# Split weights kept in DRAM and loaded again for every later use of their unit

## The chip, the cores and the metric

The kernel runs on one core of one Trainium2 chip. The metric is the device time of one execution in microseconds, lower is better. The core has TensorE (PE in the profile, with its weight loads as PEld), VectorE (DVE), ScalarE (ACT), GpSimd (POOL) and SyncE (SP); in this kernel SP issues every DMA, in the order of the program. A difference under 0.2% (2.6 us) is about what a measurement of this kernel cannot tell from none.

## The reference, cut to what matters

```
x  = linear_attention(q, k, v)                      # 4 batches, 8 heads, 576 tokens, 64 per head
p  = domain_probs / (sum(domain_probs) + 1e-9)      # [2304, 4]
y  = sum over e of p[:, e] * (relu(x @ w1[e]) @ w2[e])   # w1[e] [512, 1024], w2[e] [1024, 512], float32
h  = y @ w_in                                       # w_in [512, 2048], float64
out = (h * sigmoid(1.702 * h)) @ w_out              # w_out [2048, 512], float64; out [2304, 512]
```

x is attention's result as 2304 tokens of 512 features. The two layers after it, a mixture of four experts and a gated feed-forward layer, are nearly all of the products. The weights of the second layer arrive as float64 and are turned into float32 on the chip.

## The kernel before, in words

**Products.** A float32 operand is split into two float32r parts, `hi` (a rounded copy, made by ACT) and `lo` (operand minus `hi`, made by POOL or DVE); a product is hi*hi + hi*lo + lo*hi, three matmuls. The first product of a layer runs on 2 x 2 blocks with seven block products (Strassen's scheme in Winograd's form), so a unit of weights needs seven pieces: `a11`, `a12`, `a22`, taken from the loaded block, and `s1` to `s4`, sums and differences that POOL makes first (`sum_w`, line 481). `hi_w1` and `lo_w1` (lines 486, 490) split them; `hi_w2` and `lo_w2` (lines 494, 498) split the two halves of the second product's weights.

**Units, passes, steps.** Weights come in units of 256 hidden columns: 16 units for the experts, 8 for the feed-forward layer. Only half of the tokens (two batches, a pass) fits at once, so each layer goes over all of its units twice. A pass has two pairs of token blocks (2 x 256 and 2 x 320 tokens), and a step is one unit on one pair: the seven block products, the activation, and between them the second product of the step before. The first three units run on the first pair alone before the second pair is there, and are prepared again for the second pair. So there are 51 preparations (`insts`; 3 + 32 + 16) for 24 different units: 24 first ones and 27 repeats. Every preparation loads 1 MiB (`load_w`: `ra` and `rc`, 512 KiB each), makes four sums, seven splits and two splits, all anew.

**Order.** The opening (`START`) is a hand-written list of pieces in the order of issue. Then `step` runs five stages per step: pieces of the first product, a tile of the second product of the step before, the preparation of the next unit's weights (`prepare`, with the plan `TWO`), the second product's own weights (`hi_w2`, `lo_w2` in stages 1 and 3 of a unit's first step), and one turn of background work (`pump`). Background work is attention for the second pass's tokens during the experts' first pass, and `decode_all` during their second pass: 32 pieces of float64 weights, each loaded by SP (`w64`), turned into float32 by seven DVE operations and one POOL operation (lines 511 to 531) over four turns, and stored by SP to DRAM (line 532). The next piece's load is issued in the first of a piece's four turns, the store at the end of the last. The program's order is kept up to the second unit of the feed-forward layer (`AUTO`); after that Tile, the layer under the kernel, orders the instructions.

**Buffers.** Split pieces of the first product have 20 half-piece buffers (`w1p`), those of the second 8 (`w2p`); loaded blocks have 3 (`rawp`).

Of the kernel before, what the change touches and what calls it, by code (L numbers as in the profile page):

```python
# [8 lines left out]
F32 = mybir.dt.float32  # L9
BF16 = mybir.dt.bfloat16  # L10
F32R = mybir.dt.float32r
# [11 lines left out]
def tile_linear_attention_moe_gelu(  # L23
# [11 lines left out]
):  # L35
    """Linear attention, a mixture of experts and a gated feed-forward layer.

    A float32 operand of a product is the exact sum of two float32r parts of 12 bits, hi and lo;
    a product is hi*hi + hi*lo + lo*hi, three passes. The first product of each layer runs
    on 2 x 2 blocks with seven block products (Winograd's form of Strassen's scheme).  # L40

    Tokens of a batch are taken in the order c * 96 + p for token p * 6 + c. A pass covers two
    batches; weights come in units of 256 columns of the hidden layer.
    """
    nc = tc.nc
# [3 lines left out]
    NT, DM = out.shape  # L49
# [19 lines left out]
    accp = ctx.enter_context(tc.tile_pool(name="accp", bufs=TT))  # L69
    w1p = ctx.enter_context(tc.tile_pool(name="w1p", bufs=20))  # L70
    w2p = ctx.enter_context(tc.tile_pool(name="w2p", bufs=8))
    rawp = ctx.enter_context(tc.tile_pool(name="rawp", bufs=3))
# [38 lines left out]
    def probs_ops():  # L111
        """The normalized probabilities, each on its token's partition, as pieces by name.

        They come as [p, b, c, e]; a product with a shifted identity puts the token c * 96 + p
        into its tile of 128.
        """
        y = {}

        def pr_(_):
            n = evp.tile([SP, B, NCH, E], F32, tag="ev", name="prn")  # L120
            sh = evp.tile([SP, 3 * SP], F32, tag="ev", name="shift")
            sm = evp.tile([SP, B * NCH], F32, tag="ev", name="prs")
            y.update(sh=sh, sm=sm, f=n.rearrange("p b c e -> p (b c) e"))
            S_.dma_start(
                out=n.rearrange("p b c e -> p b (c e)"),
                in_=probs.rearrange("(b p c) e -> p b (c e)", b=B, c=NCH),
            )
            G.memset(sh, 0.0)
            G.tensor_copy(sh[:, SP : 2 * SP], ident[:SP, :SP])

        def pn(_):
            sm, f = y["sm"], y["f"]
            V.tensor_reduce(out=sm, in_=f, op=ALU.add, axis=AX.X)
            V.tensor_scalar_add(sm, sm, EPS)
            V.reciprocal(sm, sm)
            V.tensor_tensor(
                out=f, in0=f, in1=sm.unsqueeze(2).to_broadcast([SP, B * NCH, E]), op=ALU.mult
            )

        def pp(_):  # L140
            f, sh = y["f"], y["sh"]
            ps = y["ps"] = pso.tile([P, NT // P, E], F32, tag="o", name="pr_ps")
            by_tile = ps.rearrange("p (x t) e -> p x t e", t=3)
            by_group = f.rearrange("p (x g) e -> p x g e", g=4)
            for t in range(3):
                first = [(0, *divmod(t * P, SP))]
                first += [((g * SP) - t * P, g, 0) for g in range(4) if t * P < g * SP < (t + 1) * P]
                for x, (o, g, p0) in enumerate(first):
                    T.matmul(
                        by_tile[:, :, t, :], sh[:, SP + p0 - o : SP + p0 - o + P], by_group[:, :, g, :],  # L150
                        start=(x == 0), stop=(x == len(first) - 1), skip_group_check=True,
                    )

        def pc(_):
            V.tensor_copy(pr, y["ps"])

        return {"pr": pr_, "pn": pn, "pp": pp, "pc": pc}

# [1 line left out]

    KT_PATH = (0,)  # batches whose k takes its maximum on its transpose
    AHEAD = 3  # units that run on the first pair of tokens before the second is there
    LEAD = 5
# [28 lines left out]
    def attend(b, j, pool, bufs, x, small_bufs):  # L192
        """Softmax of a pair of heads and its product, x transposed into xf: its pieces by name.

        The maximum and the exponential of k are taken on k (k..) or on its transpose (K..).
        x has the tiles of k, q and v.
        """
        nm = f"{b}_{j}"
# [166 lines left out]
    def attention(todo, pool, skew):  # L365
        """Every turn a piece of each pair of heads begun; a new one every skew turns."""
        load = lambda b, j: (b, j, {x: load_attn(x, b, j, pool, 5, 2) for x in "kqv"})
# [14 lines left out]

# [1 line left out]

    X = {}

    def blocks(i, nm):
        """The seven blocks of xf[i] the products take, as pieces by name; the sums are made in place."""
        n = PAIRS[i][1]
# [31 lines left out]
    def blocks_x(g, i):  # L421
        """The blocks of the next pass, some in every stage of the steps in between."""
        ops = blocks(i, f"g{g}")
        for x in BLOCK_STAGES:
            run(ops, x)
            yield

    def to_x2(g, ti):
        """One tile of tokens of the layer's result, transposed into xf."""
        src = acc[ti]  # L430
# [10 lines left out]

# [1 line left out]

# [9 lines left out]
    insts = [*range(AHEAD), *range(NG)]  # L453
    raw, W1, W2 = {}, {}, {}

    def load_w(m, part):
        kind, e, f, *_ = units[insts[m]]
        cols = slice(f * FU, (f + 1) * FU)
# [18 lines left out]

    def sum_w(m, x):
        l, r, op = MADE[x]
        o = sump.tile([P, 2, P], F32, tag="s", name=f"{x}_{m}")  # L480
        G.tensor_tensor(out=o, in0=block_w(m, l), in1=block_w(m, r), op=op)  # L481
        sums[m, x] = o

    def hi_w1(m, x):
        W1[m, x] = tuple(w1p.tile([P, 2, P], F32R, tag="w1", name=f"{x}{r}{m}") for r in "hl")
        A.copy(W1[m, x][0], block_w(m, x))  # L486

    def lo_w1(m, x, eng):
        hi, lo = W1[m, x]
        eng.tensor_tensor(out=lo, in0=block_w(m, x), in1=hi.bitcast(F32), op=ALU.subtract)  # L490

    def hi_w2(m, c):
        W2[m, c] = tuple(w2p.tile([P, DM], F32R, tag="w2", name=f"w2{r}{m}_{c}") for r in "hl")
        A.copy(W2[m, c][0], raw[m, 1][:, c, :])  # L494

    def lo_w2(m, c, eng):
        hi, lo = W2[m, c]
        eng.tensor_tensor(out=lo, in0=raw[m, 1][:, c, :], in1=hi.bitcast(F32), op=ALU.subtract)  # L498

    def decode(src, dst, pool, nm):  # L500
        """float64 bits to the nearest float32, beyond its range clamped by the exponent."""
        n = src.shape[1]
# [28 lines left out]
        G.tensor_tensor(out=o, in0=o, in1=t.bitcast(F32), op=ALU.add)  # L531
        S_.dma_start(out=dst, in_=o)
        yield

# [1 line left out]

# [13 lines left out]
    def mm1(g, i, m, ho):  # L550
        """The first product of a layer on one block of tokens and its activation, as pieces by name."""
        n = PAIRS[i][1]
# [63 lines left out]

    # the pieces of mm1 in five stages; the last two entries run in the next step's first stage
    STAGES = {
# [5 lines left out]
    def mm2(g, ti, m, ho):  # L624
        """One tile of tokens of the second product, and its sum: as two pieces."""
        kind, e, f, pas, first, last = units[g]
# [41 lines left out]

    # what becomes of the next weights during the stages of a step, over two steps or over one
    TWO = (  # L670
# [13 lines left out]

    # the program's order is kept up to the feed-forward layer; there Tile orders it
    AUTO = 2 * NPASS * len(moe) + 2
# [18 lines left out]
    def decode_all(dec):  # L705
# [10 lines left out]
        for n, x in enumerate(todo):  # L716
            if n + 1 < len(todo):
                next(todo[n + 1])
            yield from x

    def step(k_, tiles, tail):
        """mm1 of one unit on one pair, between it the tiles of mm2 of the step before."""
        g, i, m = steps[k_]
# [34 lines left out]

    # The beginning up to the second step of the second pair, in the order of issue: piece:whose@engine;
    # _b_j is a pair of heads, a number alone a unit's weights, b a pair's blocks, s a step.  # L760
    # A bare number is so many products that keep TensorE's clock up.
    START = """
# [53 lines left out]
    def keep_warm(n):  # L816
        """TensorE's clock drops when it idles; it is kept up through the waits of the beginning."""
        for _ in range(n):
            T.matmul(hot, warm, warm, start=True, stop=True)
# [96 lines left out]
```

## Time and profile before

| | |
|---|---|
| three timed runs | 1308.29, 1309.29, 1311.00 us; median 1309.29 |
| profiled execution, first to last instruction (its own time) | 1308.0 us |
| busy: PE, PEld | 1243.1 us (95%), 1097.3 us (84%) |
| busy: DVE, ACT, POOL | 1018.5 us (78%), 585.6 us (45%), 715.4 us (55%) |
| chain of work that ended last | PE 62%, DVE 31%, issue 3%, POOL 2%, ACT 1% |
| moved by DMA | 98.85 MB, mean 76 GB/s |

Busy times of the engines overlap. The span falls into an opening (up to about 140 us), the experts' first pass (to 477), their second (to 898), and the feed-forward layer's two passes (to 1104, and to the end); where one pass gives over to the next, new blocks of the moving operand are made. A row of the view by windows gives, for one stretch, the busy time of each engine with the count of its instructions, the granted TensorE clock as a share of full speed, the mean busy share of the DMA engines, and what they moved. Matmuls are pipelined and their ends are modelled, so PE busy all the time can still be PE below its best rate.

### The profile page before, as it was taken

The page shows a single profiled execution, that of the slowest core. Times are in us where ns is not written, and L with a number is a line of the kernel's source. Part 1 is how long each engine was busy: PE and PEld are TensorE (multiplying, and loading weights), DVE is VectorE, ACT ScalarE, POOL GpSimd, SP SyncE. Part 2 cuts the span into 40 slices and gives each one's busy share as a digit, 9 for nine tenths or more (in the row PEclk, how much of TensorE's full clock was granted, in tenths as well). Part 3 has the DMA queues.
Part 4 walks back from the last instruction along what each step waited for, and adds up shares of the span by engine and source line. Part 5 has one row for each costly group of instructions (what it writes and reads, how often), then busy time and mean ns, then how long its engine had stood idle before and what let it go on. Part 6 is the DMA issues. An engine that isn't in the chain of part 4 may idle for free.

```text
span 1308.0 us, 20206 instructions
## 1 busy us (share of the span) xinstructions
PE 1243.1 (95%) x7313; PEld 1097.3 (84%) x7313; DVE 1018.5 (78%) x1721; ACT 585.6 (45%) x1468; POOL 715.4 (55%) x755
## 2 busy tenths in 40 slices
PE   8788999999999998999999999999999998999998
PEld 7677888889888987888878787898799996899997
DVE  7997776666676587999999999758666669566765
ACT  4564344344433455433333333335754555654542
POOL 5686545444454475756665566547653558354430
PEclk9899999999999998999999999999999999999999
DMA  9324222222210112334433333111120112220102
GB/s 196 104 65 125 59 76 60 60 76 77 60 49 33 49 65 81 105 121 118 125 113 115 111 121 105 65 49 33 49 65 33 50 49 65 73 65 33 40 10 73
DMA packets 82899, 98.85 MB, mean 76 GB/s; under 512 B 27760, under 2 KB 59248, under 8 KB 82800
## 3 DMA queue, kind: packets, MB, share of 16 engines
q1 hardware_dynamic: 82800, 97.57, 25.8%
q8 instruction: 57, 0.93, 0.3%
q14 instruction: 42, 0.34, 0.1%
HBM read 84.45 MB, written 13.11 MB: 75 GB/s over the span
## 4 chain that ended last, share of the span: by engine, by line
PE 62%; DVE 31%; issue 3%; POOL 2%; ACT 1%; SPq 1%; DMA 0%; POOLq 0%; DVEq 0%; ACTq 0%
PE po L639 32%; PE px L544 16%; PE pz L544 8%; DVE acc L651 6%; DVE h_lo L596 6%; PE py L544 4%; DVE u L574 2%; PE p L341 1%; DVE dso L511 1%; DVE p L574 1%; DVE dso L519 1%; DVE dto L526 1%; DVE dti L526 1%; PE px L319 1%; DVE dsi L511 1%
## 5 line engine op out<-in xcount | busy, mean ns | idle before, releaser
L639 PE MATMUL po<-w2h,h_lo 128*128 128x512 f32 x864 | 340.6, 394 | 18.2 <-DVE h_lo L596 15.6
L639 PE MATMUL po<-w2h,h_hi 128*128 128x512 f32 x864 | 343.2, 397 | 5.9 <-DVE acc L651 3.5
L639 PE MATMUL po<-w2l,h_hi 128*128 128x512 f32 x864 | 343.7, 398 | 1.2 <-POOL w2l L498 1.2
L651 DVE SCALAR_TENSOR_TENSOR acc<-po,pr,acc 128x512 f32<-128x512 f32 x270 | 200.7, 744 | 85.8 <-PE po L639 85.2
L639 PEld LDWEIGHTS po<-w2h,h_lo 128*128 128x128 f32 x864 | 163.0, 189 | 63.9 <-DVE h_lo L596 23.8
L498 POOL TENSOR_TENSOR w2l<-rc,w2h 128x512 fp32r<-128x512 f32 x98 | 136.4, 1398 | 132.5 <-ACT w2h L494 132.5
L639 PEld LDWEIGHTS po<-w2h,h_hi 128*128 128x128 f32 x864 | 163.5, 189 | 28.9 <-DVE acc L651 4.1
L639 PEld LDWEIGHTS po<-w2l,h_hi 128*128 128x128 f32 x864 | 163.7, 189 | 23.6 <-POOL w2l L498 5.7
L93 ACT COPY u<-px 128x256 f32<-128x256 f32 (+1 forms) x186 | 73.9, 397 | 229.1 <-PE px L544 228.8
L574 DVE TENSOR_TENSOR u<-pz,u 128x256 f32<-128x256 f32 (+1 forms) x192 | 86.6, 451 | 57.9 <-ACT u L93 43.0
L660 DVE TENSOR_TENSOR acc<-po,acc 128x512 f32<-128x512 f32 x126 | 86.5, 687 | 49.9 <-PE po L639 49.9
L590 ACT ACTIVATE h_hi<-u 128x320 fp32r<-128x320 f32 (+1 forms) x128 | 57.0, 445 | 96.6 <-DVE u L574 96.5
L596 DVE SCALAR_TENSOR_TENSOR h_lo<-u,h_hi 128x320 fp32r<-128x320 f32 (+1 forms) x128 | 93.2, 728 | 2.8 <-ACT h_hi L590 2.7
L481 POOL TENSOR_TENSOR s<-ra 128x256 f32<-128x256 f32 x102 | 86.2, 845 | 3.7 <-DVE s1l L490 1.7
L93 ACT COPY p<-px 128x320 f32<-128x320 f32 x93 | 36.9, 397 | 100.4 <-PE px L544 100.3
L490 POOL TENSOR_TENSOR s1l<-s,s1h 128x256 fp32r<-128x256 f32 x49 | 41.2, 842 | 73.3 <-ACT s1h L486 73.3
L490 POOL TENSOR_TENSOR a11l<-ra,a11h 128x256 fp32r<-128x256 f32 x50 | 40.8, 815 | 70.1 <-ACT a11h L486 70.0
L490 POOL TENSOR_TENSOR s2l<-s,s2h 128x256 fp32r<-128x256 f32 x49 | 42.4, 866 | 56.6 <-ACT s2h L486 55.9
L494 ACT CAST w2h<-rc 128x512 fp32r<-128x512 f32 x102 | 62.6, 619 | 14.5 <-PE po L639 14.5
L596 DVE SCALAR_TENSOR_TENSOR h_lo<-p,h_hi 128x256 fp32r<-128x256 f32 (+1 forms) x64 | 48.7, 761 | 21.1 <-ACT h_hi L590 21.0
L490 POOL TENSOR_TENSOR s3l<-s,s3h 128x256 fp32r<-128x256 f32 x47 | 41.4, 881 | 43.0 <-ACT s3h L486 41.0
L408 POOL TENSOR_TENSOR xf<-xf 128x512 f32<-128x512 f32 (+1 forms) x28 | 48.3, 1724 | 21.2 <-DVE b11lg L404 10.9
(246 smaller groups left out, 3483.2 us busy)
## 6 DMA issues: line engine op xcount, KB each, us to landing
ra<-in_moe_w SPq DMA_DIRECT2D x35, 512.0 KB, 3.6
rc<-in_moe_w SPq DMA_DIRECT2D x35, 512.0 KB, 4.0
w64i<-in_moe_w_in SPq DMA_DIRECT2D x16, 512.0 KB, 5.0
w64o<-in_moe_w_out SPq DMA_DIRECT2D x16, 512.0 KB, 4.3
ra<-wi SPq DMA_DIRECT2D x16, 512.0 KB, 3.4
rc<-wo SPq DMA_DIRECT2D x16, 512.0 KB, 3.5
q<-in_q SPq DMA_DIRECT2D x16, 288.0 KB, 5.4
v<-in_v SPq DMA_DIRECT2D x32, 144.0 KB, 5.6
```

What stands on the lines that cost most here:

```text
L93: (eng.copy if eng is A else eng.tensor_copy)(o, i)
L481: G.tensor_tensor(out=o, in0=block_w(m, l), in1=block_w(m, r), op=op)
L490: eng.tensor_tensor(out=lo, in0=block_w(m, x), in1=hi.bitcast(F32), op=ALU.subtract)
L494: A.copy(W2[m, c][0], raw[m, 1][:, c, :])
L498: eng.tensor_tensor(out=lo, in0=raw[m, 1][:, c, :], in1=hi.bitcast(F32), op=ALU.subtract)
L544: T.matmul(ps, a[:, kk, :], b[:, kk, :], start=(start and n == 0), stop=(stop and n == 5), skip_group_check=True,)
L574: return lambda _: V.tensor_tensor(out=y[o], in0=y[ps], in1=y[o], op=ALU.add)
L590: A.activation(hi, y[c], AF.Relu)
L596: V.scalar_tensor_tensor(out=lo, in0=y[c], scalar=0.0, in1=hi.bitcast(F32), op0=ALU.max, op1=ALU.subtract)
L639: T.matmul(ps, a, b, start=(n == 0), stop=(n == 3 * FT - 1))
L651: V.scalar_tensor_tensor(out=acc[ti], in0=ps, scalar=pe, in1=acc[ti], op0=ALU.mult, op1=ALU.add)
L660: V.tensor_tensor(out=acc[ti], in0=ps, in1=acc[ti], op=ALU.add)
```

## The change

The first time a unit is prepared, each split piece (`hi` and `lo` side by side in one tile) is also stored to a DRAM tile of its own. Every later preparation of the same unit allocates the same tile and fills it with one DMA load; the loading of the raw block, the four sums, the seven splits and the two splits are left out. Stores wait in a list: the oldest is issued when more than two are waiting (more than seven for the first three units), and all are issued before any load of a kept piece. The buffers stay of the same size (10 whole pieces instead of 20 halves, 4 instead of 8).

In `decode_all` the store of a decoded piece is issued by SP two turns later, in the next piece's third turn, and the next piece's load in a piece's fourth turn, where it was in its first.

```diff
+    of_unit = [units[g][:3] for g in insts]
+    again = [u in of_unit[:m] for m, u in enumerate(of_unit)]
+    kept, stores = {}, []
+
+    def new_part(m, x, pool, tag, shape):
+        t = pool.tile([P, 2, *shape], F32R, tag=tag, name=f"{x}_{m}")
+        flat = t.rearrange("p l a b -> p (l a b)").bitcast(F32)
+        u = of_unit[m]
+        if again[m]:
+            put_away(0)
+            S_.dma_start(out=flat, in_=kept[u, x])
+        else:
+            parts[m, x] = flat
+        return t[:, 0], t[:, 1]
+
+    def store_part(m, x):
+        d = dram.tile(list(parts[m, x].shape), F32, name=f"k_{x}_{m}")
+        stores.append((d, parts.pop((m, x))))
+        kept[of_unit[m], x] = d
+        put_away(7 if m < AHEAD else 2)
+
+    def put_away(but):
+        while len(stores) > but:
+            d, flat = stores.pop(0)
+            S_.dma_start(out=d, in_=flat)
 
     def load_w(m, part):
+        if again[m]:
+            return
...
     def hi_w1(m, x):
-        W1[m, x] = tuple(w1p.tile([P, 2, P], F32R, tag="w1", name=f"{x}{r}{m}") for r in "hl")
-        A.copy(W1[m, x][0], block_w(m, x))
+        W1[m, x] = new_part(m, x, w1p, "w1", [2, P])
+        if not again[m]:
+            A.copy(W1[m, x][0], block_w(m, x))
 
     def lo_w1(m, x, eng):
+        if again[m]:
+            return
         hi, lo = W1[m, x]
         eng.tensor_tensor(out=lo, in0=block_w(m, x), in1=hi.bitcast(F32), op=ALU.subtract)
+        store_part(m, x)
...
         G.tensor_tensor(out=o, in0=o, in1=t.bitcast(F32), op=ALU.add)
-        S_.dma_start(out=dst, in_=o)
+        late.append(lambda: S_.dma_start(out=dst, in_=o))
         yield
...
         for n, x in enumerate(todo):
-            if n + 1 < len(todo):
-                next(todo[n + 1])
-            yield from x
+            for stage, _ in enumerate(x):
+                yield
+                if stage == 1 and late:
+                    late.pop(0)()
+                if stage == 2 and n + 1 < len(todo):
+                    next(todo[n + 1])
+        late.pop(0)()
```

`sum_w`, `hi_w2` and `lo_w2` are changed in the same way as their neighbours.

## Rows read from the trace of the kernel before

**Rows 1.** Windows, all engines: experts' first pass, decoding stretch, rest of second pass

```profile
139.50:453.00 313.50, 310.60 (x1857) 277.83 (x1856) 217.63 (x379) 126.93 (x328) 144.38 (x173) 1.00 0.21 58
527.60:827.00 299.40, 281.06 (x1586) 242.24 (x1585) 295.02 (x464) 99.85 (x265) 188.32 (x179) 1.00 0.37 116
827.00:898.00 71.00, 71.00 (x418) 64.06 (x417) 45.30 (x75) 28.02 (x73) 38.29 (x44) 1.00 0.15 49
```

**Rows 2.** Timeline of PE: first matmul of seven steps (start, duration in us)

```profile
476.74 0.28 PE L544 MATMUL px<-b11hg,a11h 128*128 128x256 f32 x1
...
515.51 0.36 PE L544 MATMUL px<-b11hg,a11h 128*128 128x256 f32 x1
...
527.56 0.30 PE L544 MATMUL px<-b11hg,a11h 128*128 128x320 f32 x1
...
826.99 0.28 PE L544 MATMUL px<-b11hg,a11h 128*128 128x256 f32 x1
...
850.61 0.28 PE L544 MATMUL px<-b11hg,a11h 128*128 128x256 f32 x1
...
1075.69 0.28 PE L544 MATMUL px<-b11hg,a11h 128*128 128x256 f32 x1
...
1119.61 0.30 PE L544 MATMUL px<-b11hg,a11h 128*128 128x320 f32 x1
```

**Rows 3.** DVE groups, 527.6 to 827 us: count, busy us, mean ns, idle before

```profile
L596 DVE SCALAR_TENSOR_TENSOR h_lo<-p,h_hi 128x256 fp32r<-128x256 f32 x11 | 16.6, 1508 | 0.0
L512 DVE TENSOR_SCALAR dso<-dso 128x512 int32<-128x512 int32 x16 | 15.8, 986 | 0.5
L526 DVE TENSOR_TENSOR dto<-dto,dso 128x512 int32<-128x512 int32 x16 | 15.3, 954 | 0.5
...
L511 DVE TENSOR_SCALAR dso<-w64o 128x512 int32<-128x512 int32 x16 | 13.1, 821 | 0.0
...
L596 DVE SCALAR_TENSOR_TENSOR h_lo<-px,h_hi 128x256 fp32r<-128x256 f32 x12 | 4.9, 411 | 0.0
```

**Rows 4.** Three DVE lines of decoding, same stretch: shortest, median, longest ns

```profile
L511 DVE TENSOR_SCALAR dso<-w64o x16: 522/867/1078, 660.7 to 817.6; 128x512 int32<-128x512 int32 x16
...
L512 DVE TENSOR_SCALAR dsi<-dsi x12: 429/846/1410, 536.4 to 651.6; 128x512 int32<-128x512 int32 x12
...
L526 DVE TENSOR_TENSOR dto<-dto,dso x16: 692/1110/1112, 667.1 to 824.0; 128x512 int32<-128x512 int32 x16
```

**Rows 5.** Windows of line 490 alone (DVE if any, POOL, clock, DMA)

```profile
77.00:120.00 43.00, 6.61 (x10) 10.24 (x12) 1.00 0.25 76
476.70:515.50 38.80, 0.00 (x0) 7.63 (x9) 0.91 0.20 68
527.60:827.00 299.40, 0.00 (x0) 73.00 (x81) 1.00 0.37 116
...
1075.70:1119.60 43.90, 0.00 (x0) 8.23 (x8) 0.96 0.22 67
```

**Rows 6.** Windows of line 498 (DVE, POOL), then line 481 (POOL), decoding stretch

```profile
527.60:827.00 299.40, 0.00 (x0) 35.41 (x23) 1.00 0.37 116
...
527.60:827.00 299.40, 45.35 (x46) 1.00 0.37 116
```

**Rows 7.** Windows, all engines: part of the opening, two changes of pass

```profile
77.00:120.00 43.00, 35.23 (x196) 29.55 (x195) 40.00 (x59) 24.62 (x60) 36.70 (x35) 1.00 0.25 76
...
475.00:515.00 40.00, 33.22 (x180) 28.48 (x179) 34.81 (x48) 21.26 (x47) 26.87 (x22) 0.91 0.18 61
...
1076.00:1120.00 44.00, 38.92 (x212) 32.60 (x212) 41.31 (x63) 24.75 (x60) 29.11 (x24) 0.96 0.23 69
```

**Rows 8.** Waits of SP's queue, 527.6 to 827: us, times, longest

```profile
SPq L532 <- POOL doo L531: 127.7, 15, 11.3
```

**Rows 9.** DMA issues by line: count, KB each, median us to landing

```profile
rc<-in_moe_w SPq DMA_DIRECT2D x35, 512.0 KB, 4.0
w64i<-in_moe_w_in SPq DMA_DIRECT2D x16, 512.0 KB, 5.0
```

More of the change, by code (lines that the diff above doesn't have):

```diff
@@ L69, in tile_linear_attention_moe_gelu @@
     accp = ctx.enter_context(tc.tile_pool(name="accp", bufs=TT))
-    w1p = ctx.enter_context(tc.tile_pool(name="w1p", bufs=20))
-    w2p = ctx.enter_context(tc.tile_pool(name="w2p", bufs=8))
+    w1p = ctx.enter_context(tc.tile_pool(name="w1p", bufs=10))
+    w2p = ctx.enter_context(tc.tile_pool(name="w2p", bufs=4))
     rawp = ctx.enter_context(tc.tile_pool(name="rawp", bufs=3))
@@ L454, in tile_linear_attention_moe_gelu @@
     raw, W1, W2 = {}, {}, {}
+    of_unit = [units[g][:3] for g in insts]
[11 more added lines that the diff above has]
+        return t[:, 0], t[:, 1]
+    parts = {}
+    def store_part(m, x):
[7 more added lines that the diff above has]
+            S_.dma_start(out=d, in_=flat)
     def load_w(m, part):
+        if again[m]:
+            return
         kind, e, f, *_ = units[insts[m]]
@@ L484, in hi_w1 @@
     def hi_w1(m, x):
-        W1[m, x] = tuple(w1p.tile([P, 2, P], F32R, tag="w1", name=f"{x}{r}{m}") for r in "hl")
-        A.copy(W1[m, x][0], block_w(m, x))
+        W1[m, x] = new_part(m, x, w1p, "w1", [2, P])
+        if not again[m]:
+            A.copy(W1[m, x][0], block_w(m, x))
     def lo_w1(m, x, eng):
+        if again[m]:
+            return
         hi, lo = W1[m, x]
         eng.tensor_tensor(out=lo, in0=block_w(m, x), in1=hi.bitcast(F32), op=ALU.subtract)
+        store_part(m, x)
     def hi_w2(m, c):
-        W2[m, c] = tuple(w2p.tile([P, DM], F32R, tag="w2", name=f"w2{r}{m}_{c}") for r in "hl")
-        A.copy(W2[m, c][0], raw[m, 1][:, c, :])
+        hi, lo = new_part(m, f"w2{c}", w2p, "w2", [1, DM])
+        W2[m, c] = hi[:, 0], lo[:, 0]
+        if not again[m]:
+            A.copy(W2[m, c][0], raw[m, 1][:, c, :])
     def lo_w2(m, c, eng):
+        if again[m]:
+            return
         hi, lo = W2[m, c]
         eng.tensor_tensor(out=lo, in0=raw[m, 1][:, c, :], in1=hi.bitcast(F32), op=ALU.subtract)
+        store_part(m, f"w2{c}")
+    late = []
     def decode(src, dst, pool, nm):
```

## The prediction

> **What bounds the kernel now.** I read the windows first. In the experts' first pass PE is busy 310.6 of 313.5 us while DVE is at 217.6; in the rest of the second pass, 827 to 898 us, PE is busy throughout [rows 1]. There TensorE is the bound, and nothing that other engines are spared can shorten it. In the decoding stretch, 527.6 to 827 us, DVE is busy 295.0 of 299.4 us: DVE is the bound there [rows 1]. How much PE loses is read from the starts of the steps. From 826.99 to 850.61, with PE full, two steps take 23.62 us, 11.81 each. From 527.56 to 826.99 there are 23 steps: 299.43 us against 23 x 11.81 = 271.6, so 27.8 us are lost. The change from the first to the second pass (476.74 to 515.51, two steps) takes 38.77, 15.1 over; that between the feed-forward passes (1075.69 to 1119.61, three steps) 43.92 against 35.4, 8.5 over [rows 2]. In these two, and in 77 to 120 us of the opening, DVE is busy 34.8 of 40, 41.3 of 44 and 40.0 of 43 us [rows 7].
>
> In the decoding stretch PE's own busy time shows a loss of only 299.4 - 281.1 = 18.3 us [rows 1]. The Trainium skill (Perfetto Trace Analysis, Identifying the Most-Contended Engine) says that matmul busy time is a bad measure of what is left, matmuls being pipelined, and that the busy share of the weight loads should be read instead. By that rule, with PEld at 242.24/299.4 = 0.809 here and 64.06/71.0 = 0.902 where PE is full [rows 1], some 31 us are lost; the step starts agree with it, not with the 18. With 18 the gain below would be 15 instead of 23 and the time 1284.
>
> The next view is the list of DVE groups. The same subtraction `h_lo` on 256 columns takes 1508 ns when its operand is `p`, in SBUF, and 411 ns when it is `px`, in PSUM [rows 3]. Decoding's line 512 takes 986 ns on average and 429 at its shortest, line 526 954 against 692, line 511 821 against 522 [rows 3, 4]. These operations stand until a POOL operation has ended. Waiting is thus 0.56 + 0.26 + 0.30 = 1.12 us per decoded piece, 32 us over the stretch's 29 pieces, and 1.10 x 11 = 12 us on `h_lo`: 44 us of DVE's 295, a floor, since the other decoding lines are left out.
>
> **The change part by part.**
>
> *Weights of the repeats.* Of POOL's 188.3 us in the decoding stretch, preparing weights is 73.0 (splits of the first product), 35.4 (of the second) and 45.4 (sums), together 153.8 or 82% [rows 1, 5, 6]. All of that stretch's units are repeats, so all of it goes; so do ACT's copies, which cost nothing there since ACT is busy a third of the time. DVE loses at least 0.82 x 44 = 36 us and needs at most 259 us, under PE's 271.6: PE becomes the bound. What is late next is `h_lo`, where it meets the 18% of POOL's work that stays, decoding's own line 531. I let the loss shrink with the waits: 27.8 x 0.82 = 23 us. Ends: 28 if PE runs full; 12 if 259 us of DVE work in bursts still leave PE half of its loss.
>
> *Change of pass at 477 us.* Units 0 and 1 of the second pass are prepared here, both repeats. The loss is 15.1; line 490 is 7.6 of POOL's 26.9 us, 28% [rows 5, 7], so 4 us. Ends: 0, if the chain stays on DVE's own block and decoding work; 9, if all the weights' work counts.
>
> *Change at 1076 us.* Again the next two units are repeats: 8.2 of 29.1 us, 28% of 8.5 [rows 5, 7], 2 us; ends 0 and 6. The change at 898 us prepares first uses of feed-forward units, and keeps its cost.
>
> *Opening.* The second preparation of units 0 to 2 falls in 77 to 120 us. Of ten DVE splits there (6.6 us, [rows 5]) nine go, some 6 us, with POOL's to match. DVE is the bound there [rows 7], but other chains lie beside it: 4 us. At the first repeat SP must wait for the last split of unit 2, issue the stores still waiting (up to seven of 256 KiB), and only then the loads. If PE then waits once for a block to land, it costs one landing, 4.0 us [rows 9]. Ends: -4 and 10.
>
> *Full stretches.* In both first passes the weights' work stays and stores are added: 7 pieces of 256 KiB and 2 of 512 KiB per unit, 2.9 MB. Per unit, 26 us in the first pass, that is 110 GB/s on top of 58. At 58 GB/s for a share of 0.21 [rows 1] the DMA engines would be at about 0.6, an estimate from that row. A store waits for a split two pieces back; a raw block's load waits today for later splits than that, so SP is not held longer. Buffers are used again ten pieces later, more than a unit, so no split waits for its store. Cost nothing, the cover being the step (12 us) by which raw blocks are ahead of their use; should that go, each of 21 units waits for a landing of 4.0 us. I allow up to 5 us. The Trainium skill (SBUF — State Buffer, SBUF: two separate sides) says that a DMA and an engine cannot slow each other; by that the cost is nothing, and no stretch here has PE full at such a DMA share to show it.
>
> *Loads in the second passes.* 2.9 MB per unit of 23.6 us, 122 GB/s, replace 1 MiB of raw loads, about 40: 116 becomes about 200 GB/s in the decoding stretch, a share of 0.63 by its row [rows 1]. Pieces of the first product are needed five or more stages (2.4 us each) after their issue. The closest is the second half of the second product's weights: issued in stage 3, needed in stage 0 of the next step, 4.7 us, against 4.0 us for 512 KiB to land [rows 9]. SP is ahead of its place by as much as buffers allow, three or four stages here, since these pieces' buffers are free a step earlier; that lead hides the rest.
>
> *Decoding's store and load.* SP stands 127.7 us for line 531 at the stores of `doo` alone [rows 8], with the raw loads behind it. Two turns later the POOL operation is done and SP passes. The load of the next piece moves past that store and past the kept pieces' loads of three turns; in program order it now comes one turn (2.4 us) before its use, against a landing of 5.0 us [rows 9]. It still hides if SP is two turns ahead. By its waits it can be: the w64 buffer it takes is free after line 528 of the piece before, and the store before it needs line 531 of three turns ago. I take 0; bounds 0 and the price in the second rival.
>
> *Sum.* 23 + 4 + 2 + 4 = 33 us off the profiled span of 1308.0: 1275. The median shown, 1309.29, is 1.3 above that span, which I leave as it is: 1276.3.
>
> **The rivals.** *DVE stays the bound in the decoding stretch.* For it: 259 of 271.6 us is 95% busy, and the `h_lo` that PE waits for stands in the same queue as decoding. Against it: 259 is a ceiling, as the waits were a floor, and PE ran full with DVE at 69% [rows 1]. Then 12 us there, 2 and 1 at the changes, nothing in the opening: 15 off, 1294.
>
> *SP comes too late, the other side.* One queue now carries, per unit, nine loads that wait for buffers, and decoding's loads and stores between them. Place: the decoding stretch, at `w64` and at the second product's second half. It decides where SP is less than about a turn ahead of its place, so that `w64` lands 5.0 - 2.4 = 2.6 us late. For 29 pieces that is 75 us of standing DVE; 259 + 75 = 334 against 299.4 now is 35 longer, and with 10 gained elsewhere 25: 1334. For it: the order in the program, and that a buffer wait of the stage before can hold SP. Against: today SP comes early to every store and waits there [rows 8], and the wait that held it is what moves away. The Trainium skill (DMA: Bandwidth & Descriptors, Queues, rings and completion order) adds that a transfer's completion is signalled only after earlier writes of the same DMA engine have landed; by that rule a load behind stores is told later. No stretch of this trace has the two in such number.
>
> *It cancels.* Stores in the two first passes hold raw loads and cost what the second passes gain: 21 units by 1.6 us is 33, about 1309. For it: a DMA share about three times today's. Against: a slack of a step.
>
> **How the numbers follow.** Forecast 0.70, the first rival 0.14, slower 0.11, cancelling 0.05. The forecast's own ends give 12 + 0 + 0 - 4 - 5 = 3 to 28 + 9 + 6 + 10 = 53 off if all fell on one side; not all will, so its own range is 1260 to 1290. With the first rival and part of its upper side the 80% range is 1260 to 1302. A change under 0.2%, 2.6 us, counts as none: a measurement of this kernel cannot tell it. Faster 0.70 + 0.14 = 0.84; same 0.05; slower 0.11.
>
> **What would show it.** Right: steps of about 11.8 to 12.2 us throughout the decoding stretch; POOL there down from 188 to about 35 us, DVE's lines 511 to 526 near their shortest; no wait of SP on line 531; step times unchanged in 139 to 453 and 946 to 1076 us. The first rival would show as DVE still over 95% busy there with short operations. The second would show as DVE idle before line 511, or PE before line 639, with a DMA as releaser. The prediction is wrong if steps with full PE grow in the first passes, or if the decoding stretch still takes over 290 us.

## The result and the profile after

The changed kernel takes 1274.36 us (median of four, 1269.98 to 1275.87), the kernel before beside it 1310.14 (1308.29 to 1313.2). The ratio is 0.9716, 95% interval 0.9695 to 0.9738: 2.8% faster, 2 us from the 1276.3 forecast. The profiled execution of the changed kernel is the fastest of its four: its own time is 1269.98, its span 1268.2. Of all executions behind the numbers below one, of the kernel with the real work put back, took 6863.58 us instead of about 1304; it is in no comparison.

From the page of the changed kernel: busy times of the engines, and the chain that ended last by engine.

```profile
PE 1230.9 (97%) x7313; PEld 1099.7 (87%) x7313; DVE 933.1 (74%) x1709; ACT 501.7 (40%) x1225; POOL 394.5 (31%) x416
...
PE 85%; DVE 8%; issue 2%; POOL 2%; DMA 1%; ACT 1%; SPq 1%; POOLq 0%; ACTq 0%; DVEq 0%
```

POOL's work has nearly halved (715.4 before), and DVE's share of the chain has gone from 31% to 8%.

Windows of the changed kernel: experts' first pass, decoding stretch, rest of the second pass, and the two changes of pass. Columns as in [rows 1]: stretch, length, PE, PEld, DVE, ACT, POOL, granted clock, DMA share, GB/s.

```profile
135.83:449.67 313.84, 310.69 (x1858) 277.93 (x1856) 218.35 (x379) 127.04 (x328) 144.89 (x173) 1.00 0.54 172
520.28:791.80 271.52, 271.52 (x1585) 244.91 (x1584) 245.68 (x460) 64.38 (x162) 37.66 (x29) 1.00 0.61 200
791.80:863.31 71.51, 71.11 (x416) 63.83 (x415) 41.65 (x75) 20.73 (x53) 11.33 (x12) 1.00 0.43 144
473.29:508.25 34.96, 30.45 (x176) 26.02 (x175) 31.01 (x48) 17.33 (x35) 11.33 (x7) 0.95 0.35 107
1040.03:1079.45 39.42, 36.89 (x212) 31.56 (x211) 36.59 (x63) 20.84 (x48) 13.13 (x8) 1.00 0.44 128
```

Timeline of PE in the changed kernel: the same first matmuls of steps as in [rows 2].

```profile
473.29 0.28 PE L591 MATMUL px<-b11hg,a 128*128 128x256 f32 x1
...
508.25 0.36 PE L591 MATMUL px<-b11hg,a 128*128 128x256 f32 x1
...
520.28 0.30 PE L591 MATMUL px<-b11hg,a 128*128 128x320 f32 x1
...
791.80 0.28 PE L591 MATMUL px<-b11hg,a 128*128 128x256 f32 x1
...
1040.03 0.28 PE L591 MATMUL px<-b11hg,a 128*128 128x256 f32 x1
...
1079.45 0.30 PE L591 MATMUL px<-b11hg,a 128*128 128x320 f32 x1
```

The 23 steps of the decoding stretch take 791.80 - 520.28 = 271.5 us, 27.9 less than in [rows 2]: 11.81 per step, PE busy all the time, DVE at 90%, POOL down from 188.3 to 37.7. The change of pass at 477 takes 508.25 - 473.29 = 35.0, 3.8 less; that at 1076 39.4, 4.5 less. The first pass takes 313.8 against 313.5 although the DMA share in it has gone from 0.21 to 0.54 [rows 1]. The opening ends at 135.8 against 139.5 us. 27.9 + 3.8 + 4.5 + 3.7 is 39.9; all that lies elsewhere moves by 0.1 in sum, since the spans differ by 39.8.

DVE groups of the changed kernel in 520.3 to 791.8 us, in the order of [rows 3] (line 643 is 596 of before, 559 is 512, 573 is 526, 558 is 511).

```profile
L643 DVE SCALAR_TENSOR_TENSOR h_lo<-p,h_hi 128x256 fp32r<-128x256 f32 x11 | 4.6, 419 | 0.0
...
L559 DVE TENSOR_SCALAR dso<-dso 128x512 int32<-128x512 int32 x16 | 6.8, 428 | 0.5
L573 DVE TENSOR_TENSOR dto<-dto,dso 128x512 int32<-128x512 int32 x16 | 11.1, 693 | 0.5
...
L558 DVE TENSOR_SCALAR dso<-w64o 128x512 int32<-128x512 int32 x16 | 6.6, 415 | 0.0
...
L643 DVE SCALAR_TENSOR_TENSOR h_lo<-px,h_hi 128x256 fp32r<-128x256 f32 x11 | 4.6, 414 | 0.0
```

The three decoding lines are at their shortest of before [rows 4] or under it: 986 ns became 428, 954 became 693, 821 became 415 (522 at its shortest). `h_lo` on 256 columns went from 1508 to 419 ns; there the operand in SBUF now costs no more than the one in PSUM. The same work takes DVE 245.7 us instead of 295.0.

Some groups got slower, one above all. `h_lo` on 320 columns of `p`, before and in the changed kernel, then one of these operations and the POOL operation beside it:

```profile
L596 DVE SCALAR_TENSOR_TENSOR h_lo<-p,h_hi 128x320 fp32r<-128x320 f32 x12 | 5.8, 485 | 0.0
```

```profile
L643 DVE SCALAR_TENSOR_TENSOR h_lo<-p,h_hi 128x320 fp32r<-128x320 f32 x12 | 11.1, 924 | 2.5 <-ACT h_hi L637 2.5
```

```profile
572.36 1.29 POOL L578 TENSOR_TENSOR doi<-doi,dti 128x512 f32<-128x512 f32 x1 [8.14 <-DVE doi L575]
```

```profile
572.63 1.36 DVE L643 SCALAR_TENSOR_TENSOR h_lo<-p,h_hi 128x320 fp32r<-128x320 f32 x1 [0.41 <-ACT h_hi L637]
```

POOL's operation ends at 573.65, the DVE operation beside it at 573.99. So DVE still stands for what is left of POOL's work, some 5 us in this group. It costs no time: PE waits for nothing in this stretch.

Waits of SP's queue in the changed kernel, 520.3 to 791.8 us (us, times, longest).

```profile
SPq L469 <- PE px L591: 87.3, 30, 6.8
SPq L579 <- POOL doo L578: 63.9, 13, 6.9
```

SP still waits for the POOL operation before a decoded store, half as long as in [rows 8], and otherwise for buffers. With 45.6 us at `doi` it stands there 109.5 us in all, at most 6.9 at a time; that it would no longer wait there was one of the forecast's signs, and it did not come.

### The profile page after: what moved, and what is told of

The parts are those of the page before. It is cut to its first block, busy times and chain, and to the rows that moved or that the text cites. A ratio compares the mean times of both kernels' runs of the same rounds, so it can differ in the third digit from the quotient of the medians.

```text
span 1268.2 us, 20329 instructions
## 1 busy us (share of the span) xinstructions
PE 1230.9 (97%) x7313; PEld 1099.7 (87%) x7313; DVE 933.1 (74%) x1709; ACT 501.7 (40%) x1225; POOL 394.5 (31%) x416
## 4 chain that ended last, share of the span: by engine, by line
PE 85%; DVE 8%; issue 2%; POOL 2%; DMA 1%; ACT 1%; SPq 1%; POOLq 0%; ACTq 0%; DVEq 0%
PE po L686 43%; PE px L591 22%; PE pz L591 11%; PE py L591 5%; PE p L344 1%; DVE h_lo L643 1%; PE px L322 1%; DVE acc L698 1%; POOL xf L411 1%; SPq L189 1%; DMA k_a<-a 0%; DMA q<-in_q 0%; DVE xf L411 0%; DVE dg L260 0%; POOL s L517 0%
## 5 line engine op out<-in xcount | busy, mean ns | idle before, releaser
L686 PE MATMUL po<-w,h_hi 128*128 128x512 f32 x1728 | 544.6, 396 | 4.3 <-DMA w<-k_w 1.6
L686 PEld LDWEIGHTS po<-w,h_hi 128*128 128x128 f32 x1728 | 302.7, 189 | 45.9 <-issue 1.8
L686 PE MATMUL po<-w,h_lo 128*128 128x512 f32 x864 | 337.8, 391 | 3.7 <-DVE h_lo L643 3.1
L686 PEld LDWEIGHTS po<-w,h_lo 128*128 128x128 f32 x864 | 162.8, 188 | 43.3 <-DVE h_lo L643 4.8
L529 POOL TENSOR_TENSOR s<-s,s 128x256 fp32r<-128x256 f32 x91 | 71.5, 789 | 101.2 <-ACT s L523 101.2
L542 POOL TENSOR_TENSOR w<-rc,w 128x512 fp32r<-128x512 f32 x47 | 63.6, 1357 | 67.4 <-ACT w L536 64.3
L591 PE MATMUL px<-t4hg,a 128*128 128x256 f32 (+1 forms) x256 | 62.4, 299 | 2.4 <-ACT u L96 2.4
L591 PE MATMUL pz<-b22hg,s 128*128 128x256 f32 (+1 forms) x256 | 61.8, 297 | 0.5 <-DVE u L621 0.4
L591 PE MATMUL pz<-t1hg,s 128*128 128x256 f32 (+1 forms) x256 | 62.1, 298 | 0.0
L591 PE MATMUL px<-t2hg,s 128*128 128x256 f32 (+1 forms) x256 | 61.8, 296 | 0.0
```

The costliest lines, as they stand in the source:

```text
L591: T.matmul(ps, a[:, kk, :], b[:, kk, :], start=(start and n == 0), stop=(stop and n == 5), skip_group_check=True,)
L686: T.matmul(ps, a, b, start=(n == 0), stop=(n == 3 * FT - 1))
```

## The experiments

Theory A: DVE is faster because POOL's sums and splits no longer stand beside it, and PE ran behind DVE. Rivals: ACT's copies, which went too, mattered; or the gain comes from the second part of the change, the later store and load of decoding. The forecast's price of nothing for that part and for the stores is tested as well; that the reloads cost nothing is seen above, where PE is busy all of the decoding stretch.

**The first part alone.**

```diff
-        late.append(lambda: S_.dma_start(out=dst, in_=o))
+        S_.dma_start(out=dst, in_=o)
...
-            for stage, _ in enumerate(x):
-                yield
-                if stage == 1 and late:
-                    late.pop(0)()
-                if stage == 2 and n + 1 < len(todo):
-                    next(todo[n + 1])
-        late.pop(0)()
+            if n + 1 < len(todo):
+                next(todo[n + 1])
+            yield from x
```

> The change without its second part: split weights are kept and loaded again, but a decoded piece is stored at the end of its last turn and the next piece is loaded in the first turn, as in the kernel before. Theory A (the gain is DVE no longer standing for POOL's weight work): the decoding stretch, 23 steps, stays at 272 to 276 us against 271.5 in the changed kernel and 299.4 before; total within 5 us of the changed kernel, 1270 to 1280. Rival B (the gain is SP's queue, which no longer stands at the decoded pieces' stores): the stretch returns to 290 or more, total 1290 to 1305. A third outcome, that both parts are needed since SP now stands at a store with the kept pieces' loads behind it, would show PE waiting for loaded pieces at the second product.

Measured: 1287.25 us, ratio 0.9817 (0.9792 to 0.9843), 13 us above the whole change. Its decoding stretch, by windows, PE's waits and SP's waits:

```profile
524.62:811.80 287.18, 276.83 (x1585) 247.03 (x1584) 245.42 (x460) 64.38 (x162) 37.61 (x29) 0.99 0.57 190
```

```profile
PE po L686 <- DMA w<-k_w: 10.4, 9, 1.9
```

```profile
SPq L579 <- POOL doo L578: 116.8, 16, 10.1
SPq L579 <- POOL doi L578: 96.8, 13, 10.1
```

DVE is as quick as in the changed kernel (245.4 us); yet the stretch is 15.7 us longer. SP stands 213.6 us at the decoded stores, up to 10.1 at a time, with the kept loads behind it, and PE waits for the second product's weights, 10.4 us of the 15.7. This is the third outcome of the expectation, my second rival at a lower price, and the second part of the change is what keeps it away.

**The second part alone**, on the kernel before.

```diff
-        S_.dma_start(out=dst, in_=o)
+        late.append(lambda: S_.dma_start(out=dst, in_=o))
...
+            for stage, _ in enumerate(x):
+                yield
+                if stage == 1 and late:
+                    late.pop(0)()
+                if stage == 2 and n + 1 < len(todo):
+                    next(todo[n + 1])
+        late.pop(0)()
```

> The kernel before with the second part of the change alone: decoded pieces stored two turns later, next piece loaded three turns later, weights split anew each time. Theory A: nothing is gained, the decoding stretch stays at 297 to 302 us, total 1305 to 1313. Rival B: the stretch falls to 280 or less, total 1290 or less. If the load, now one turn ahead of its use, comes late, DVE stands before its line 511 for 1 to 3 us per piece and the total is up to 1340.

Measured: 1313.26 us, ratio 1.0025 (1.0014 to 1.0036), 0.3 us over the expected range; the stretch takes 301.1 us with DVE busy 292.9. Alone it gains nothing, and may cost 3 us: its worth shows only once kept loads stand in the same queue.

**POOL's work back, without its data**: for each sum and split left out in a repeat from the second pass on, POOL subtracts a constant from itself (256 columns, two operands in SBUF, nothing waited for).

```diff
+    def idle(n=1):
+        for _ in range(n):
+            z = sump.tile([P, 2, P], F32, tag="s", name="idle")
+            b = ident.unsqueeze(1).to_broadcast([P, 2, P])
+            G.tensor_tensor(out=z, in0=b, in1=b, op=ALU.subtract)
...
         if again[m]:
+            if m >= 2 * AHEAD:
+                idle()
             return
```

> The changed kernel, and for every repeat from the second pass on POOL again does two-operand subtractions of 256 columns on constants, in the places and the number of the sums and splits that were left out; nothing reads their results, ACT's copies stay away and nothing waits for them. Theory A: the operations alone bring DVE's waits back; the decoding stretch is 292 to 302 us, decoding's line 512 of before is back near 0.8 to 1.0 us, total 1295 to 1308. Rival B and rival C (fewer copies on ACT): the stretch stays at 272 to 276 us, total 1270 to 1280.

Measured: 1331.88 us, ratio 1.0166 (1.0143 to 1.019), but not for the expected reason. The decoding stretch by windows and POOL's largest group in it, then waits from 1040 to 1120 us:

```profile
518.46:795.68 277.22, 275.88 (x1585) 243.55 (x1584) 268.94 (x461) 64.25 (x162) 162.40 (x196) 1.00 0.60 196
```

```profile
L516 POOL TENSOR_TENSOR idle<-ident 128x256 f32<-128x256 f32 x167 | 125.5, 783 | 0.0
```

```profile
ACT t1hg L403 <- POOL xf L411: 40.1, 1, 40.1
...
PE px L603 <- ACT u L96: 28.6, 1, 28.6
```

The stretch grew by 5.7 us only, against at least 20 expected: a miss. DVE is busy 23 us longer (245.7 to 268.9), and its idle tenth covered most of that. The rest of the loss is one step of 71 us at 1044 us. There the program's order is no longer kept, 90 of POOL's operations that wait for nothing run from 1022 us on ahead of the first of the next pass's blocks that POOL makes, and ACT waits 40.1 us for it. So the kernel's time says nothing on theory A; a substitute that waits for nothing is not the work.

**ACT's copies back.** The same function with `A.copy(z.bitcast(F32R), ident.unsqueeze(1).to_broadcast([P, 2, P]))`, called where a repeat leaves a copy out.

> The changed kernel, and for every repeat from the second pass on ACT again makes copies of 256 columns in the places of the nine copies that were left out; nothing reads them. Theory A: no change, decoding stretch 271.5 to 273 us, total 1270 to 1280. Rival C (the gain is ACT being quicker with the products' results): the stretch returns to 285 or more, total 1288 or more.

Measured: 1274.69 us, ratio 0.9728 (0.9708 to 0.9748), the time of the changed kernel. Decoding stretch by windows:

```profile
522.58:794.06 271.48, 271.48 (x1585) 244.88 (x1584) 245.98 (x460) 102.20 (x287) 37.65 (x29) 1.00 0.61 200
```

ACT has its 100 us again (102.2; 99.9 in [rows 1]) and PE stays full. The ACT rival falls.

**The real work back**, in units 20 to 34 of the order, which fill the decoding stretch: raw loads, sums, copies and splits are done anew in the old order and places, into tiles that nobody reads; the products use the kept pieces.

```diff
+    anew = range(4 * AHEAD + 8, AHEAD + 2 * len(moe))
...
-        if again[m]:
+        if again[m] and m not in anew:
             return
...
         if again[m]:
+            if m in anew:
+                z = side[m, x]
+                G.tensor_tensor(out=z, in0=block_w(m, x), in1=z.bitcast(F32), op=ALU.subtract)
             return
```

> The changed kernel, and for the units prepared during decoding (repeats 20 to 34) the whole work on weights is done again beside the kept pieces' loads: raw blocks loaded, four sums, nine copies on ACT, nine subtractions on POOL, in their old places and with their old waits, into scratch that nobody reads. The run before showed that the same number of POOL operations without waits costs the decoding stretch only 6 us (277), not 20 to 30. Theory A, mended (POOL's work stops DVE, but how much hangs on where its operations fall; waiting for ACT spreads them between DVE's): the stretch goes back to 288 to 300 us, DVE over 97% busy, total 1291 to 1303. Rival D (the rest of the loss was not DVE's waits but somebody waiting for POOL's results): the stretch stays at 272 to 279, total 1274 to 1282. If instead SP is held at raw loads, PE waits for kept pieces by DMA, and that part is not theory A's.

Measured: 1304.33 us, ratio 0.9951 (0.9933 to 0.9968), 1 us over the expected range. Decoding stretch by windows, PE's largest wait in it, and the first row of [rows 3]:

```profile
520.37:819.65 299.28, 279.36 (x1585) 242.71 (x1584) 294.44 (x466) 99.61 (x265) 187.34 (x177) 1.00 0.65 224
```

```profile
PE po L700 <- DVE h_lo L657: 15.5, 17, 1.4
```

```profile
L657 DVE SCALAR_TENSOR_TENSOR h_lo<-p,h_hi 128x256 fp32r<-128x256 f32 x11 | 15.5, 1406 | 0.0
```

These are the numbers of [rows 1] again: 299.3 us, DVE 294.4, POOL 187.3, although all pieces come from DRAM and the DMA share is 0.65. The whole gain of the stretch goes with the POOL work beside DVE (ACT's being cleared by the run above), and PE now waits for `h_lo`, which stands again (1406 ns, 1508 before). The raw loads that were put back with it do not explain the loss: PE waits for no DMA there, DVE 1.8 us. Theory A holds.

**POOL writes only**: a memset of 768 columns in each of those places.

```diff
+            z = side["dec"].tile([P, 768], F32, tag="z", bufs=1, name="idle")
+            G.memset(z, 0.0)
```

> The changed kernel with a POOL memset of 768 columns (about 0.8 us, it reads nothing) in each place of a sum or split left out, during decoding alone; so many POOL operations as in e3_pool_work_back, but write-only. If any POOL operation stops DVE, decoding's lines stand as in e3_pool_work_back (line 512 of before 0.72 us, line 519 0.91, line 526 0.75) and the stretch is 276 to 278. If DVE operations with two operands in SBUF stand only for a POOL operation that reads, lines 519 and 526 and the h_lo of u are at their shortest (0.69, 0.69, 0.7) and only one-operand lines 511 and 512 stand; stretch 271.5 to 275.

Measured in a single execution: 1286.8 us. The stretch takes 284.4 us, longer than either expectation had it, and PE waits 6.8 us for `h_lo`. The stretch by windows, then four groups of DVE in it:

```profile
522.60:806.95 284.35, 277.29 (x1586) 243.26 (x1584) 277.23 (x460) 64.44 (x162) 171.61 (x197) 1.00 0.58 191
```

```profile
L571 DVE TENSOR_SCALAR dso<-w64o 128x512 int32<-128x512 int32 x16 | 16.6, 1036 | 0.0
L572 DVE TENSOR_SCALAR dso<-dso 128x512 int32<-128x512 int32 x16 | 14.8, 923 | 0.6
L586 DVE TENSOR_TENSOR dto<-dto,dso 128x512 int32<-128x512 int32 x16 | 11.1, 693 | 0.5
L579 DVE SCALAR_TENSOR_TENSOR dso<-w64o,dso 128x512 int32<-128x512 int32 x16 | 11.1, 693 | 0.6
```

Two kinds of standing come apart. The two lines with two operands in SBUF are untouched (693 ns, their shortest), while those with one stand about as long as beside the real work (1036 and 923, against 821 and 986 in [rows 3]). So "POOL is busy" is not one cost. The Trainium skill (SBUF — State Buffer, Who interferes with whom) has it that a VectorE instruction with two SBUF inputs contends with a GpSimd instruction that reads SBUF, not with one that only writes it, and that forms which can use both port pairs, `tensor_scalar` among them, can contend with GpSimd; these four rows agree.

**The opening anew**: units 0 to 2 are split again for the second pair, and stored then.

```diff
-    again = [u in of_unit[:m] for m, u in enumerate(of_unit)]
+    again = [m >= 2 * AHEAD and u in of_unit[:m] for m, u in enumerate(of_unit)]
...
+        if m < AHEAD:
+            return
...
-        put_away(7 if m < AHEAD else 2)
+        put_away(7 if m < 2 * AHEAD else 2)
```

> The changed kernel, but units 0 to 2 are split anew for the second pair of tokens in the opening, as before; they are stored then, and the second pass still loads them. If the opening's gain is real (3.7 us in the one profile of the changed kernel), the step at 136 us starts at 139 to 140, and the total is 1276 to 1280. If it was chance, the total stays at 1272 to 1276, as the changed kernel.

Measured: 1283.34 us, ratio 0.979 (0.9767 to 0.9812), and an opening that ends at 147.4 us, 8 later than before the change; both expectations missed it. It is no clean undoing: the stores now fall into the stretch that is split anew, ACT waits there for stores to free buffers (7.5 us in two waits), and PE 7.6 us for DVE's `acc`. It shows that reloading in the opening costs less than splitting and storing there; the gain over the kernel before is not told apart by it.

**Decoding starts ten turns later**, so that it no longer lies in the change of pass.

```diff
+        yield from [None] * 10
         next(todo[0])
```

> The changed kernel with decoding begun ten turns (two steps) later. With the weights' work gone DVE has room in the decoding stretch, and none in the change of pass at 473 us, where decoding's first pieces stand between the blocks' operations. Theory A: the two steps of the change, 35.0 us in the changed kernel, fall to 27 to 32 and nothing is lost later; total 1266 to 1272. If the change of pass hangs on the blocks' chain on POOL and ACT alone, it stays at 34 to 36 and the total at 1272 to 1276.

Measured: 1264.41 us, ratio 0.9648 (0.9627 to 0.9668). It beats both kernels. The change of pass by windows (the changed kernel's row is the fourth of the first windows above):

```profile
476.70:505.00 28.30, 28.02 (x177) 24.74 (x175) 20.36 (x32) 17.47 (x35) 9.31 (x5) 1.00 0.37 124
```

6.7 us shorter, DVE at 20.4 instead of 31.0: of the 11.3 us that these two steps still took over two full ones (23.6), 6.7 were decoding on DVE, not weights; the other 4.7 are not explained. Its decoding stretch stays at 271.5. The two profiled executions differ by 1.7 us only, as its opening ended 3.6 later in this one and the change at 898 took 1.5 more. The 10 us between the medians are thus explained to 6.7. The rest is not shown in a trace: the other executions of this kernel took 1263.3 to 1265.5 us at a mean granted clock of 0.993 (this one 0.989), those of the changed kernel 1273.9 to 1275.9 at 0.987 and 0.988 (the profiled one 0.990), so that how their openings ran (below) may be part of it.

**Store late, load early**: the store's delay alone.

```diff
+            if n + 1 < len(todo):
+                next(todo[n + 1])
             for stage, _ in enumerate(x):
...
-                if stage == 2 and n + 1 < len(todo):
-                    next(todo[n + 1])
```

> The changed kernel with half of its second part: a decoded piece is stored two turns later, as in the change, but the next piece is loaded in a piece's first turn, as before. e1_decode_as_before (both as before) cost 16 us in the decoding stretch, PE waiting for kept pieces' loads. Theory E (SP stood at the store for line 531's result, with the kept pieces' loads behind it): the late store alone is enough, stretch 271.5 to 273, PE waits for a kept piece under 3 us in all, total 1271 to 1277. Rival F (the decoded pieces' loads, early in the queue, are what the kept pieces wait behind): stretch 280 to 287, total 1282 to 1290.

Measured: 1271.78 us, ratio 0.9719 (0.9694 to 0.9743). Decoding stretch by windows:

```profile
520.36:791.90 271.54, 271.54 (x1585) 244.66 (x1584) 245.49 (x460) 64.36 (x162) 37.63 (x29) 1.00 0.61 200
```

The same to 0.1 us. Of the second part it is the store's delay that counts; where the next piece's load stands makes no difference.

**Every store twice**, the second time to a tile that nobody reads.

```diff
             S_.dma_start(out=d, in_=flat)
+            S_.dma_start(out=spare[id(d)], in_=flat)
```

> The changed kernel with every kept piece stored twice, to two DRAM tiles. The prediction put the stores at nothing in the stretches where PE is full, at a DMA share that they bring from 0.21 to 0.54 in the experts' first pass. Theory A: doubled, with a share of 0.8 to 0.95, the 23 steps from 150 to 450 us still take the same 300 us within 1, the feed-forward layer's first pass too; the opening, where SP's queue is short of time, may lose 0 to 6 us; total 1272 to 1282. Rival (stores do hold SP or the DMA engines): the first pass grows by 10 us or more, total 1285 or more.

Measured: 1283.94 us, ratio 0.9804 (0.9783 to 0.9825), 2 us above what was expected at most. First pass by windows, and PE's wait in the opening (90 to 110 us):

```profile
145.95:459.00 313.05, 310.83 (x1861) 278.41 (x1860) 217.31 (x380) 127.23 (x328) 144.38 (x173) 1.00 0.82 284
```

```profile
PE px L593 <- DMA a<-k_a: 6.8, 1, 6.8
```

By the starts of the steps the 26 steps from the end of the opening to the change of pass take 336.3 us, 337.5 in the changed kernel, at a DMA share of 0.82: there the stores are free with room to spare. 10.1 us of the loss lie in the opening, where PE waits for the first kept pieces.

**Fewer stores waiting**, on the kernel whose decoding starts later.

```diff
-        put_away(7 if m < AHEAD else 2)
+        put_away(2)
```

> The kernel whose decoding starts ten turns later, with one more edit: in the first three units too, a store is issued as soon as more than two are waiting (it was more than seven), so that at most two, not seven, stand before the first load of a kept piece. With every store doubled, the opening had been 10 us longer and PE had waited 6.8 us for the first kept piece there, so the waiting stores have a price. Theory A: that price is paid by the single stores too; five fewer of them before the first load give back 2 to 5 us in the opening: 1259 to 1263. Theory B: the seven wait for a reason; stores issued earlier make the queue stand at a split of the opening with loads of attention and of raw blocks behind it, and the opening grows by 2 to 8 us: 1266 to 1272. If neither, the time stays within 2 us of 1264.4, and the doubled stores' 10 us were due to their number alone.

Measured: 1264.16 us, ratio 0.9654 (0.9633 to 0.9676): neither theory, no change. The number of stores in the opening has a price when doubled; the place of five of them has none.

**Where the opening varies.** Eight of these profiles hold the same opening, and it ends between 134.0 and 140.2 us. One wait tells much of it. PE's timeline in the changed kernel, then in the one whose decoding starts later (start, duration, in brackets the idle time before and what ended it):

```profile
124.45 0.47 PE L686 MATMUL po<-w,h_hi 128*128 128x512 f32 x1 [1.60 <-DMA w<-k_w]
```

```profile
126.50 0.47 PE L686 MATMUL po<-w,h_hi 128*128 128x512 f32 x1 [3.85 <-DMA w<-k_w]
```

SP's timeline in the changed kernel (start, duration of the issue), and windows of the other execution around that wait:

```profile
119.56 1.01 SPq L469 DMA_DIRECT2D w<-k_w  x2
```

```profile
120.73:128.00 7.27, 3.42 (x19) 2.89 (x18) 1.48 (x3) 0.81 (x3) 0.00 (x0) 0.93 1.03 296
128.00:132.00 4.00, 4.00 (x19) 3.67 (x18) 1.24 (x2) 1.50 (x4) 2.30 (x4) 0.70 1.02 240
```

The kept pieces of a second product are issued at 119.6, when PE has freed their buffer (SP waits up to 7.5 us for that), and needed at 122.9, with the DMA engines full. Where PE's wait was 3.85 us, the granted clock fell to 0.70 in the next 4 us, that is, part of them at 1.2 instead of 2.4 GHz, and the step took 18.7 us instead of 14.9; where it was 4.4, in the run of the first part alone, 20.1. All eight go this way: behind the three longest waits (2.4, 3.85 and 4.4 us) the clock granted from 128 to 132 us was 0.78, 0.70 and 0.53, and these openings end at 139.4 us or later; behind the five others (1.6 to 2.3 us) it was 1.00, and they end by 136.2. That 3.8 us separates these two executions is shown; that the wait alone makes the clock fall is read from these traces, not tested.

## Why the prediction was right

*What bounded.* Right. PE was behind DVE in the decoding stretch, DVE behind POOL: the real work put back in that stretch alone gives back 27.8 of its 27.9 us. The loss was 28 us, as the step starts said (31 by the weight loads), and not the 18 of PE's busy time. The rule that I took from the Trainium skill (Perfetto Trace Analysis, Identifying the Most-Contended Engine) is borne out here: the weight loads' share rose from 0.81 to 0.90 when the loss was gone.

*Decoding stretch: 23 forecast, 27.9 measured.* The term was mis-sized, at the step 27.8 x 0.82: I let the loss shrink in proportion to POOL's work, as if each microsecond of it cost the same. But the lines that I had counted lost all of their standing, 44.5 us and not 36 (93.1 us before, 48.6 in the changed kernel), and decoding's other lines lost some 15 that I had not counted; DVE came to 245.7 us, 13 under my ceiling of 259. And a DVE that is 10% idle no longer delays PE at all. `h_lo` beside decoding's own POOL operation, which I named as late next, is there (924 ns), but PE does not wait for it. POOL's substitute shows the same from the other side: 23 us more of DVE cost PE 5.7, the real work's 49 cost it 27.8.

*Change at 477: 4 forecast, 3.8 measured.* POOL's work there fell from 26.9 [rows 7] to 11.3 us, by all of the weights' work and not by line 490's share, from which I had the 4; that the number came out may be luck. Of what was left, 6.7 us are shown to be decoding on DVE by starting it later. *Change at 1076: 2 forecast, 4.5 measured*, by the same share and inside its ends; why twice as much was not tested.

*Opening: 4 forecast, 3.7 in the profiled execution.* Over eight profiles with this opening it ends at 137.0 on average, against 139.7 in two of before's: 2.8. Three of the eight end where these two do, so that a gain here is likely but not clear of the spread, and that the splits left out are its reason was not isolated. The single wait for a landing that I put in as an end is there in all eight, 1.6 to 4.4 us.

*Full stretches: nothing, and right*, with the doubled stores as the test; the row that was missing for the Trainium skill's rule on DMA and engines (SBUF — State Buffer, SBUF: two separate sides) is there now, and it agrees: PE busy 310.8 of 313.1 us at a DMA share of 0.82. The 5 us that I allowed did not follow from my own condition: 21 landings of 4.0 us are 84. *Decoding's store and load: nothing, right as a change by itself, wrong in its weight.* I had SP pass the store two turns later; it still stands there 109.5 us, but at most 6.9 at a time against 10.1, and PE does not notice. I priced the second rival at 75 us of late `w64` loads. Of the two places that I named for it the other one decides, the second product's kept pieces, held behind the decoded store. It costs 15.7 us without the store's delay and nothing with it. Where `w64` is loaded made no difference once the store was late.

*The sum.* 33 forecast; 39.8 between the two profiled executions, 35.8 between the medians. The 4 us between these are the changed kernel's profiled execution, 4.4 below its median. So the sum came nearer to the medians than its largest term to its stretch, and that in part by luck: by the profiled executions it is 7 us short.

## What to carry to other kernels

A DVE row that is far above the same form's shortest, or above the same operation with its operand in PSUM, can be POOL's cost written in DVE's name, as it was here; the timelines of both engines show it. Work taken off POOL is then worth what DVE had stood beside it, and PE gains of it what it had stood behind DVE. Here PE lost 10% of the stretch with DVE busy 98% of it, 5% and 2% beside the two substitutes with DVE at 97%, and nothing at 90%. When work is replaced by loads, look at what else stands in the queue that issues them: here a store that waited for a result held the loads behind it, and delaying the store by two turns was worth 13 us. Then look again at what the remaining background work collides with: moving its start by ten turns gave another 10 us.

## What the runs showed of the hardware that was not expected

What POOL costs DVE is not a matter of its busy time alone: 125 us of small operations that wait for nothing cost DVE 23 us, 150 us of the real work 49. Whether the shapes or the spacing make the difference was not told apart. Memsets cost DVE 32 us with both two-operand rows above at their shortest. What stays of POOL's work moves its cost to other lines: with the weights' work gone, `h_lo` on 320 columns took 924 ns instead of 485. And an opening with the same instructions ended up to 6 us apart between executions, in good part at one load that came 1.6 to 4.4 us late and, behind the three longest of these waits, at a granted clock of 0.53 to 0.78 for four us.
